# One core, layer norm + linear attention + MLP: the written order of all engines laid out anew from the third K product on

## The chip, the cores and the metric

One core of one Trainium2 chip. The metric is the device time of one execution in microseconds (us), the median over runs. Profiles show one profiled execution, with times from its first instruction.

## The reference

2048 rows of 512 features in bf16, 32 heads of 16, a hidden layer of 1792:

```python
def _A_ref(x, wqkv, wo):
    qkv = (x @ wqkv).reshape(B, S, 3, H, Dh).transpose(2, 0, 3, 1, 4)
    q, k, v = qkv[0], qkv[1], qkv[2]
    phi = lambda t: jnp.where(t > 0, t + 1, jnp.exp(t)) + 1e-6
    pq, pk = phi(q), phi(k)
    kv = jnp.einsum("bhsd,bhse->bhde", pk, v)
    z = jnp.einsum("bhsd->bhd", pk)
    num = jnp.einsum("bhqd,bhde->bhqe", pq, kv)
    den = jnp.einsum("bhqd,bhd->bhq", pq, z)[..., None] + 1e-6
    return (num / den).transpose(0, 2, 1, 3).reshape(B, S, D) @ wo
...
h = x + _A_ref(_layernorm(x), A_wqkv, A_wo)
h2 = h + relu(_layernorm(h) @ B_w1) @ B_w2
```

## The kernel before

The rows are cut into 16 tiles t of 128 rows, and four tiles make a chunk c of 512 columns for the transposed side. Nothing is planned at run time: the whole program is one list of words, ORDER, and a loop at the end calls for each word the function op_name with its numbers. A word stands for the work of one engine, and each engine runs its own words in the order of the list. Semaphores between engines are put in from the data that words share, also where a word writes a buffer that an earlier word has still to read. So moving a word changes what it stands behind on its own engine, and nothing else.

The words by stage (number after the name: tile, chunk and column block; the last number is often the PSUM bank or how many blocks the word covers):

- Loads on SyncE's queue: lx (x, L201), lk, lq, lv, lo, l1, l2 (weights, L204).
- First layer norm: S, A on VectorE (statistics, L222, L223), R on ScalarE (two instructions, L228), N on VectorE (L247). Its transpose into lnT is either T on TensorE with E on ScalarE (L266, L276), or X, a DMA transpose on SyncE (L287). One chunk's four tiles share one lnT.
- K products: K on TensorE, four matmuls (L295); phi in parts: F (exp) and U (relu) on ScalarE (L313, L316), M (min) and D (add) on VectorE (L320, L323). W (L328) does U and D in one VectorE instruction that reads PSUM. Then G on TensorE (L347) sums ln'phi(k) over the tiles into banks 4 to 7, and za, zf, z, zc, zh make the row sums z.
- Q products: Q (L303), with qF, qU, qM, qD, qW as for K, into pqT, one per chunk.
- gA (ScalarE, L380) or gD (VectorE, L383) copy G's banks, two at a time, into gT; kv (L388), kx (L396), m (L400) and mA (L403) make the matrix that stands for kv and wo together.
- Denominator of chunk c: dn on TensorE (16 small matmuls, L444), dnl (Ln, L450) and dnx (Exp spread over 16 columns, L457) on ScalarE, into rn, which is wk_sb used again. Per tile it is transposed into rd by dt, a DMA transpose on SyncE (L476), or by rt on TensorE (L266) with a copy by re on ScalarE (L468) or rv on VectorE (L472). dm on VectorE (L480) multiplies pqT with rd into pqs. rd exists once: dt of the next chunk writes what dm of this chunk reads. For chunk 0 the tiles 0, 1 and 2 go by dt, tile 3 by rt.
- h on TensorE (L490), hD on VectorE (L496, adds x); second layer norm s, a, r, n; x, a DMA transpose on SyncE (L288), back into lnT.
- MLP: p on TensorE (L506, first product), pA on ScalarE or pD on VectorE (relu, L512, L517), two banks each; f on TensorE (L526, second product, in two halves of seven), fo on VectorE (L534, adds h), fd the store (SyncE). There are two buffers for the hidden activations, for even and odd chunks.

All eight PSUM banks are one tile named bk, and a word's bank number says which bank it takes. The last tile's second product, f.15, is cut in three column pieces (15.3.1, 15.0.2, 15.2.1), each with its own fo and fd.

```python
    op_X = lambda t: nc.sync.dma_start_transpose(out=lnT_of(t), in_=ln_nat[:, t, :])
...
    def op_dt(t):
        j = t % CT
        nc.sync.dma_start_transpose(out=rd[:, :, j * P : (j + 1) * P], in_=rn[:, j, :])
...
    for word in ORDER.split():
        name, *idx = word.split(".")
        ops[name](*map(int, idx))
```

Of the kernel before, what the change touches and what calls it, by code (L numbers as in the profile page):

```python
# [16 lines left out]

ORDER = """
const table lx.0.1 lx.2.1 S.0 lx.1.1 S.2 A.0 S.1 A.2 R.0.1 N.0 R.2.1 lx.3.1 lk.0.2 lx.4.2 warm.1.7 warm.9.7
A.1 R.1.1 T.0.6 S.3 N.2 N.1 A.3 E.0 lk.2.2 warm.1.7 R.3.1 S.4 T.2.7 lx.6.2 E.2 N.3 S.5 T.1.4 A.4 K.0.1 E.1 A.5  # L20
F.0.1 R.4.2 S.6 T.3.2 K.1.0 M.0.1 E.3 U.0.1 lx.8.4 K.2.3 F.1.1 N.5 masks U.1.1 N.4 S.7 D.0.1 M.1.1 A.7 A.6
R.6.2 D.1.1 K.3.2 F.2.1 F.3.1 U.2.1 U.3.1 S.9 N.6 lx.12.4 X.5 G.0 X.4 G.1 M.2.1 A.9 S.8 N.7 A.8 M.3.1 D.2.1
R.8.2 K.5.1 lq.0.2 D.3.1 N.9 K.4.0 F.4.2 X.6 S.13 N.8 X.7 G.2 A.13 S.12 M.4.2 X.9 A.12 G.3 U.4.2 R.12.2 K.6.2
X.8 D.4.2 K.7.3 N.12 S.10 S.11 N.13 G.4 K.9.1 K.8.0 F.6.2 U.6.2 A.11 M.6.2 A.10 X.12 R.10.2 D.6.2 X.13 N.11
S.15 N.10 A.15 za.2 U.8.2 F.8.2 S.14 M.8.2 A.14 G.5 G.6 G.7 X.11 K.12.0 X.10 K.13.1 K.11.3 R.14.2 lq.2.2 za.4
N.14 D.8.2 K.10.2 N.15 za.6 X.14 F.12.2 U.12.2 X.15 F.10.2 G.8 Q.0.0.0 Q.0.1.1 M.12.2 lv.2.2 l1.0.2 l1.2.2
lo.0.4 lv.0.2 U.10.2 K.14.2 G.9 K.15.3 D.12.2 M.10.2 za.8 D.10.2 qU.0.0.2 G.10 za.10 qF.0.0.2 F.14.2 qM.0.0.2
za.12 Q.0.2.0 Q.0.3.1 G.11 M.14.2 zf.12 qF.0.2.2 G.12 W.14.2 qM.0.2.2 l2.7.7 qD.0.0.2 G.13 z.1.2.14 z.3.2.14
z.2.2.14 z.0.2.14 zc qW.0.2.2 G.14 G.15 zh dn.0.0 dnl.0 dnx.0.0.2 gD.2.2 gD.0.2 Q.1.0.2 Q.1.1.3 Q.1.3.1 kv.2.4
kv.3.4 dnx.0.3.1 dnx.0.2.1 kv.1.4 kv.0.4 Q.1.2.0 kx qF.1.0.2 qU.1.0.2 m.0.4 rt.3.3 m.2.6 m.1.5 Q.2.0.2 m.3.7  # L30
dt.1 qM.1.0.2 qF.1.2.2 dt.0 dt.2 re.3 qD.1.0.2 Q.2.1.3 mA.0.2 qM.1.2.2 l2.0.7 mA.2.2 qW.1.2.2 dn.1.5 dm.0.0.2
Q.2.3.1 dnl.1 dnx.1.0.2 dm.0.2.2 h.3.5 hD.3 dnx.1.2.2 qF.2.0.2 qU.2.0.2 s.3 h.1.4 hD.1 a.3 s.1 h.0.5 Q.2.2.0
n.3 hD.0 dt.5 dt.6 h.2.4 qU.2.2.2 qF.2.2.2 a.1 s.0 dt.7 hD.2 n.1 s.2 a.0 n.0 dt.4 dm.1.0.2 Q.3.0.2 Q.3.1.3
Q.3.3.1 Q.3.2.0 dm.1.2.2 a.2 x.3 h.4.6 h.7.4 qU.3.0.2 qF.3.0.2 x.1 h.6.5 h.5.7 qF.3.2.2 n.2 qM.2.2.2 qM.2.0.2
qD.2.0.2 qM.3.0.2 qD.2.2.2 x.0 dn.2.3 x.2 dnl.2 dnx.2.2.2 p.0.0.2 p.0.1.3 hD.4 qM.3.2.2 qW.3.2.2 qD.3.0.2
pD.0.0.2 hD.7 hD.5 dnx.2.0.2 p.0.3.1 dn.3.6 p.0.2.0 dt.10 dt.11 hD.6 s.5 s.4 dt.8 dt.9 p.0.5.3 p.0.4.2
dm.2.2.2 s.7 a.7 dm.2.0.2 r.0.4 pA.0.2.2 dnl.3 pA.0.4.2 p.0.7.1 p.0.6.0 dnx.3.2.2 pA.0.6.2 p.0.13.3 f.0.4.0.7
p.0.12.2 pA.0.12.2 f.1.5.0.7 h.9.3 h.10.1 h.11.0 h.8.6 dnx.3.0.2 a.4 s.6 hD.9 a.5 a.6 hD.10 hD.11 p.0.9.3
p.0.11.1 p.0.8.2 p.0.10.0 dt.14 dt.13 dt.15 f.3.7.0.7 pA.0.10.2 pA.0.8.2 n.5 dt.12 n.6 dm.3.0.2 dm.3.2.2 n.4
s.11 n.7 hD.8 h.14.1 h.13.3 f.0.4.7.7 h.12.0 h.15.6 hD.14 s.10 s.8 s.14 hD.12 s.9 x.5 x.7 x.6 x.4 f.1.5.7.7  # L40
f.3.7.7.7 fo.0 hD.15 p.1.9.1 p.1.8.0 f.2.6.0.7 pA.1.8.2 f.2.6.7.7 p.1.0.0 p.1.1.1 fo.1 a.14 a.10 a.8 fo.3 s.12
a.11 a.12 s.15 a.15 n.11 hD.13 s.13 a.13 a.9 n.8 n.10 p.1.3.3 n.9 n.12 pA.1.0.2 fo.2 x.10 fd.3 x.9 x.8 x.11
p.1.10.6 p.1.4.0 p.1.7.5 fd.0 p.1.5.1 p.1.2.2 p.1.11.7 p.1.6.4 n.14 pD.1.6.2 r.12.4 pA.1.4.2 n.15 n.13
pD.1.10.2 pA.1.2.2 p.2.4.0 p.2.5.1 pA.2.4.2 x.15 f.5.5.0.7 p.2.0.0 p.2.1.1 p.2.2.2 p.2.3.3 pA.2.0.2 p.1.13.1
f.7.7.0.7 p.1.12.0 f.4.4.0.7 pD.2.2.2 pD.1.12.2 p.2.7.3 p.2.6.2 p.2.13.1 f.6.6.0.7 f.7.7.7.7 f.5.5.7.7
p.2.12.0 r.4.4 pD.2.6.2 p.2.10.2 f.6.6.7.7 pA.2.12.2 x.12 x.14 x.13 fd.1 fd.2 p.2.9.1 p.2.11.3 p.2.8.0 fo.7
pA.2.10.2 pD.2.8.2 f.4.4.7.7 p.3.3.3 p.3.9.1 p.3.8.0 fo.4 pA.3.8.2 fo.5 fo.6 f.8.4.0.7 p.3.5.1 p.3.4.0 p.3.2.2
f.9.5.0.7 pD.3.4.2 pD.3.2.2 fd.5 fd.4 p.3.0.0 f.10.6.0.7 f.9.5.7.7 f.10.6.7.7 p.3.6.2 p.3.7.3 p.3.1.1 fd.6
f.8.4.7.7 pD.3.6.2 pA.3.0.2 r.8.4 fo.9 fo.10 p.3.13.1 f.11.7.0.7 p.3.11.3 p.3.12.0 pA.3.12.2 fo.8 f.11.7.7.7
fd.7 fd.9 p.3.10.2 f.12.4.0.7 f.14.6.0.7 fo.11 pD.3.10.2 f.15.5.0.14.3.1 f.12.4.7.7 f.14.6.7.7 fd.8 fd.10  # L50
fd.11 fo.15.3.1 fo.12 fo.14 f.13.5.0.7 f.13.5.7.7 fo.13 f.15.7.0.14.0.2 fd.12 fd.14 fd.13 fd.15.3.1
f.15.4.0.14.2.1 fo.15.0.2 fd.15.0.2 fo.15.2.1 fd.15.2.1
"""


# [521 lines left out]
```

## Time and profile before

| | |
|---|---|
| median of 3 runs | 170.41 us (170.32 to 170.6) |
| the profiled execution | 171.34 us, of which the span is 169.6 |
| TensorE (PE), matmuls | 162.6 us busy, 96% of the span |
| VectorE (DVE) | 102.6 us, 61% |
| ScalarE (ACT) | 65.2 us, 38% |
| GpSimd (POOL) | 4.9 us, 3% |
| DMA engines | 15.75 MB, mean 93 GB/s |
| mean granted TensorE clock | 1.000 |

The page gives busy time, the chain that ended last, and groups of instructions by line. In the chain and the timeline a row is: start, duration, what. PEld is the loading of weights, which goes beside the matmuls; SPq is SyncE's queue, where DMAs are issued one after the other. Of the DMA queues, q1 carries the kernel's transfers, and q8 and q14 carry packets of instructions for the engines' own fetching: seven of 16 KB on q8, 19 to 28 us apart in this trace, and four smaller ones on q14. A DMA's row on SPq is its issue alone; its landing is told in the DMA view as time from issue to landing.

### The profile page before, as it was taken

What the parts mean: (1) busy time and instruction counts of PE and PEld (TensorE: products, weight loads), DVE (VectorE), ACT (ScalarE), POOL (GpSimd) and SP (SyncE); (2) the same over time, 40 slices, a digit from 0 to 9 for tenths busy, and PEclk for the clock granted to TensorE, in tenths of its full rate; (3) what the DMA queues carried; (4) which work ended last, traced back from release to release, by engine and by line L of the source; (5) the groups of instructions that cost most, each with busy time, mean ns of one, the idle gap of its engine ahead of it and who ended that gap; (6) DMA issues with size and microseconds to landing.
All of it is one profiled execution on the core that took longest, in us unless ns stands there. A gap on an engine that the chain in (4) does not pass through costs nothing.

```text
span 169.6 us, 2272 instructions
## 1 busy us (share of the span) xinstructions
PE 162.6 (96%) x847; PEld 75.6 (45%) x863; DVE 102.6 (61%) x203; ACT 65.2 (38%) x98; POOL 4.9 (3%) x21
## 2 busy tenths in 40 slices
PE   7879989999999999999999999999999999999993
PEld 2334434445544354444444444444444444444553
DVE  3979999998678999545888903324204250344232
ACT  3868767741998827740400134320022200301000
POOL 7400000000000000000000000000000000000000
PEclk9999999999999999999999999999999999999999
DMA  4955545898357533314370052340000300020012
GB/s 128 312 192 142 110 81 125 270 395 261 65 122 203 108 64 66 62 31 95 60 69 0 9 115 62 69 120 1 0 0 0 124 0 4 0 93 31 0 66 62
DMA packets 31675, 15.75 MB, mean 93 GB/s; under 512 B 24240, under 2 KB 30640, under 8 KB 31664
## 3 DMA queue, kind: packets, MB, share of 16 engines
q1 hardware_dynamic: 31664, 15.61, 36.1%
q8 instruction: 7, 0.11, 0.3%
q14 instruction: 4, 0.03, 0.1%
HBM read 7.86 MB, written 2.10 MB: 59 GB/s over the span
## 4 chain that ended last, share of the span: by engine, by line
PE 83%; DMA 7%; DVE 5%; SPq 2%; issue 2%; ACT 0%; DVEq 0%
PE bk L526 28%; PE bk L506 28%; PE bk L490 9%; PE bk L303 6%; PE bk L347 6%; PE bk L295 4%; DMA x_nat<-in_A_x_dram 3%; DMA lnT<-h_nat 2%; DVE st L222 2%; DMA rd<-wk_sb 2%; SPq L201 1%; DVE h_nat L247 1%; DVE eb L320 1%; PE bk L444 1%; PE bk L388 1%
## 5 line engine op out<-in xcount | busy, mean ns | idle before, releaser
L526 PE MATMUL bk<-w_sb,at 128*128 128x512 bf16 (+2 forms) x248 | 51.2, 355 | 0.2
L506 PE MATMUL bk<-lnT,w_sb 128*128 128x512 bf16 x220 | 50.9, 380 | 0.2
L512 ACT ACTIVATE at<-bk 128x1024 bf16<-128x1024 f32 x17 | 17.2, 1022 | 67.3 <-PE bk L506 60.9
L526 PEld LDWEIGHTS <-at 128*128 128x128 bf16 x252 | 23.5, 98 | 25.2
L506 PEld LDWEIGHTS <-w_sb 128*128 128x128 bf16 x224 | 21.7, 98 | 26.0
L517 DVE TENSOR_SCALAR at<-bk 128x1024 bf16<-128x1024 f32 x11 | 13.4, 1223 | 32.7 <-PE bk L506 32.6
L534 DVE SCALAR_TENSOR_TENSOR gT<-bk,rstd,h_nat 128x512 bf16<-128x512 f32 (+2 forms) x18 | 12.0, 688 | 15.9 <-PE bk L526 14.8
L313 ACT ACTIVATE eb<-bk 128x1024 bf16<-128x1024 f32 (+1 forms) x18 | 16.4, 924 | 4.0 <-PE bk L295 2.4
L295 PE MATMUL bk<-wk_sb,lnT 128*128 128x512 bf16 x63 | 15.3, 380 | 0.7 <-DMA lnT<-h_nat 0.5
L490 PE MATMUL bk<-m_sb,pqs 128*128 128x512 bf16 x61 | 15.1, 380 | 0.2
L303 PE MATMUL bk<-lnT,wq_sb 128*128 128x512 bf16 x61 | 14.6, 379 | 0.1
L496 DVE TENSOR_TENSOR h_nat<-bk,x_nat 128x512 bf16<-128x512 f32 x16 | 10.8, 684 | 4.7 <-PE bk L490 4.7
L316 ACT ACTIVATE rb<-bk 128x1024 bf16<-128x1024 f32 (+1 forms) x14 | 12.5, 901 | 2.6 <-PE bk L303 1.9
L347 PE MATMUL bk<-at,h_nat 128*128 128x512 bf16 x56 | 13.4, 379 | 0.1
L222 DVE BATCH_NORM_STATS2 st<-x_nat 128x6 f32<-128x512 bf16 x16 | 10.7, 677 | 3.1 <-DMA x_nat<-in_A_x_dram 3.1
L224 DVE BATCH_NORM_STATS2 st<-h_nat 128x6 f32<-128x512 bf16 x16 | 10.7, 682 | 0.1
L347 PEld LDWEIGHTS <-h_nat 128*128 128x128 bf16 x64 | 6.2, 98 | 8.7 <-issue 1.5
L490 PEld LDWEIGHTS <-pqs 128*128 128x128 bf16 x64 | 5.9, 98 | 8.7 <-DVE pqs L480 2.0
L295 PEld LDWEIGHTS <-lnT 128*128 128x128 bf16 x64 | 6.0, 98 | 8.3 <-DMA lnT<-h_nat 1.4
L303 PEld LDWEIGHTS <-wq_sb 128*128 128x128 bf16 x64 | 6.1, 97 | 6.9
L457 ACT ACTIVATE wk_sb<-ld 128x1024 bf16<-128x1024 f32 (+1 forms) x9 | 8.2, 951 | 0.1
L480 DVE TENSOR_TENSOR pqs<-pqT,rd 128x1024 bf16<-128x1024 bf16 x8 | 5.2, 685 | 4.4 <-DMA rd<-wk_sb 2.6
(57 smaller groups left out, 89.9 us busy)
## 6 DMA issues: line engine op xcount, KB each, us to landing
w_sb<-in_B_w_dram SPq DMA_DIRECT2D x4, 896.0 KB, 5.8
out_dram<-gT SPq DMA_DIRECT2D x15, 128.0 KB, 1.9
x_nat<-in_A_x_dram SPq DMA_DIRECT2D x2, 512.0 KB, 7.5
x_nat<-in_A_x_dram SPq DMA_DIRECT2D x4, 128.0 KB, 2.3
wk_sb<-in_A_wqkv_dram SPq DMA_DIRECT2D x2, 256.0 KB, 3.3
...
```

The lines of the kernel that those rows point to most:

```text
L222: op_S = lambda t: nc.vector.bn_stats(out=st[:, t, :], in_=x_nat[:, t, :])
L295: nc.tensor.matmul(bk[:, b, :], lhsT=lnT[c][:, kd, j * P : (j + 1) * P], rhs=wk_sb[:, kd, :], start=(kd == 0), stop=(kd == KD - 1),)
L303: nc.tensor.matmul(bk[:, b, :], lhsT=wq_sb[:, kd, j * P : (j + 1) * P], rhs=lnT[c][:, kd, :], start=(kd == 0), stop=(kd == KD - 1),)
L313: nc.scalar.activation(out=buf(eb, kind, i, n), in_=bank(at_bank[kind, i], n), func=ACT.Exp)
L316: nc.scalar.activation(out=buf(rb, kind, i, n), in_=bank(at_bank[kind, i], n), func=ACT.Relu)
L347: nc.tensor.matmul(bk[:, KD + kd, :], lhsT=ln_nat[:, t, kd * P : (kd + 1) * P], rhs=pk(t)[:, 0, :], start=(t == 0), stop=(t == NT - 1),)
L490: nc.tensor.matmul(bk[:, b, :], lhsT=pqs[:, (c * KD + jb) % NQ, j * P : (j + 1) * P], rhs=m_sb[:, jb, :], start=(jb == 0), stop=(jb == KD ...
L506: nc.tensor.matmul(bk[:, b, cols], lhsT=w1_sb[:, kd, f * P : (f + 1) * P], rhs=lnT[c][:, kd, cols], start=(kd == 0), stop=(kd == KD - 1),)
L512: nc.scalar.activation(out=acts[c % 2][:, f : f + n, :], in_=bank(at_bank["p", c, f], n), func=ACT.Relu)
L517: nc.vector.tensor_scalar(out=acts[c % 2][:, f : f + n, :], in0=bank(at_bank["p", c, f], n), scalar1=0.0, scalar2=None, op0=ALU.max,)
L526: nc.tensor.matmul(bk[:, b, 0 : w * P], lhsT=acts[c % 2][:, f, j * P : (j + 1) * P], rhs=w2_sb[:, f, k * P : (k + w) * P], start=(f == 0), ...
L534: nc.vector.scalar_tensor_tensor(out=o_t[:, t % NO, cols], in0=bk[:, at_bank["f", t, k], 0 : w * P], scalar=rstd2[:, t : t + 1], in1=h_nat ...
```

## The change

ORDER is replaced from the word after K.0.1 on (the warm-up, the first transposes and K.0 stay; masks, which is GpSimd's own, is called earlier). A function op_warmq is added that no word calls. The matmuls are the same ones in another order, some in other banks. Twenty pieces of elementwise work change engine or form: W.6.2 for U.6.2 and D.6.2; U.14.2 and D.14.2 for W.14.2; qU.0.2.2 and qD.0.2.2 for qW.0.2.2; gA.0.2 for gD.0.2; rv.3 for re.3; and fifteen of the relu words of the MLP go from pA to pD or back. On SyncE, lx.12.4 goes before lx.8.4, lq.2.2, lq.0.2 and lv.2.2 go among other transposes, and both l2 loads before l1. The diff, the old lines up to the second chunk's denominators and the new ones up to the MLP's first product; of the rest, four new lines:

```diff
-A.1 R.1.1 T.0.6 S.3 N.2 N.1 A.3 E.0 lk.2.2 warm.1.7 R.3.1 S.4 T.2.7 lx.6.2 E.2 N.3 S.5 T.1.4 A.4 K.0.1 E.1 A.5
-F.0.1 R.4.2 S.6 T.3.2 K.1.0 M.0.1 E.3 U.0.1 lx.8.4 K.2.3 F.1.1 N.5 masks U.1.1 N.4 S.7 D.0.1 M.1.1 A.7 A.6
-R.6.2 D.1.1 K.3.2 F.2.1 F.3.1 U.2.1 U.3.1 S.9 N.6 lx.12.4 X.5 G.0 X.4 G.1 M.2.1 A.9 S.8 N.7 A.8 M.3.1 D.2.1
-R.8.2 K.5.1 lq.0.2 D.3.1 N.9 K.4.0 F.4.2 X.6 S.13 N.8 X.7 G.2 A.13 S.12 M.4.2 X.9 A.12 G.3 U.4.2 R.12.2 K.6.2
-X.8 D.4.2 K.7.3 N.12 S.10 S.11 N.13 G.4 K.9.1 K.8.0 F.6.2 U.6.2 A.11 M.6.2 A.10 X.12 R.10.2 D.6.2 X.13 N.11
-S.15 N.10 A.15 za.2 U.8.2 F.8.2 S.14 M.8.2 A.14 G.5 G.6 G.7 X.11 K.12.0 X.10 K.13.1 K.11.3 R.14.2 lq.2.2 za.4
-N.14 D.8.2 K.10.2 N.15 za.6 X.14 F.12.2 U.12.2 X.15 F.10.2 G.8 Q.0.0.0 Q.0.1.1 M.12.2 lv.2.2 l1.0.2 l1.2.2
-lo.0.4 lv.0.2 U.10.2 K.14.2 G.9 K.15.3 D.12.2 M.10.2 za.8 D.10.2 qU.0.0.2 G.10 za.10 qF.0.0.2 F.14.2 qM.0.0.2
-za.12 Q.0.2.0 Q.0.3.1 G.11 M.14.2 zf.12 qF.0.2.2 G.12 W.14.2 qM.0.2.2 l2.7.7 qD.0.0.2 G.13 z.1.2.14 z.3.2.14
-z.2.2.14 z.0.2.14 zc qW.0.2.2 G.14 G.15 zh dn.0.0 dnl.0 dnx.0.0.2 gD.2.2 gD.0.2 Q.1.0.2 Q.1.1.3 Q.1.3.1 kv.2.4
-kv.3.4 dnx.0.3.1 dnx.0.2.1 kv.1.4 kv.0.4 Q.1.2.0 kx qF.1.0.2 qU.1.0.2 m.0.4 rt.3.3 m.2.6 m.1.5 Q.2.0.2 m.3.7
-dt.1 qM.1.0.2 qF.1.2.2 dt.0 dt.2 re.3 qD.1.0.2 Q.2.1.3 mA.0.2 qM.1.2.2 l2.0.7 mA.2.2 qW.1.2.2 dn.1.5 dm.0.0.2
-Q.2.3.1 dnl.1 dnx.1.0.2 dm.0.2.2 h.3.5 hD.3 dnx.1.2.2 qF.2.0.2 qU.2.0.2 s.3 h.1.4 hD.1 a.3 s.1 h.0.5 Q.2.2.0
...
+A.1 R.1.1 T.0.6 S.3 N.2 N.1 masks A.3 E.0 lk.2.2 warm.1.7 R.3.1 S.4 T.2.7 lx.6.2 E.2 N.3 S.5 T.1.4 A.4 K.0.1
+E.1 lx.12.4 lx.8.4 K.2.3 T.3.0 A.5 F.0.1 R.4.2 S.6 E.3 M.0.1 N.5 U.0.1 X.5 K.1.2 S.7 D.0.1 F.1.1 K.3.0 A.7 A.6
+N.4 G.0 M.1.1 U.1.1 D.1.1 R.6.2 U.3.1 U.2.1 N.7 S.9 F.3.1 F.2.1 S.8 N.6 A.9 A.8 M.3.1 G.1 X.4 M.2.1 X.7 D.3.1
+X.6 R.8.2 D.2.1 N.9 N.8 S.12 S.13 K.5.1 S.10 A.13 A.12 K.4.0 G.2 X.9 X.8 F.4.2 U.4.2 R.12.2 K.7.3 K.6.2 G.3
+M.4.2 S.11 N.12 D.4.2 K.9.1 F.6.2 G.4 K.8.0 A.11 A.10 M.6.2 S.15 N.13 R.10.2 F.8.2 U.8.2 W.6.2 X.12 N.10 S.14
+N.11 A.14 M.8.2 A.15 D.8.2 lv.2.2 lq.2.2 X.13 G.5 X.10 X.11 lq.0.2 R.14.2 N.15 N.14 za.2 G.6 G.7 K.12.0 G.8
+za.4 K.13.1 K.10.2 K.11.3 F.12.2 U.12.2 G.9 F.10.2 X.15 X.14 U.10.2 Q.0.0.0 Q.0.1.1 qF.0.0.2 M.12.2 za.6 za.8
+qU.0.0.2 M.10.2 D.12.2 D.10.2 K.15.3 K.14.2 G.10 Q.0.3.1 Q.0.2.0 qM.0.0.2 G.11 lo.0.4 l2.7.7 lv.0.2 l2.0.7
+U.14.2 F.14.2 G.12 za.10 za.12 qF.0.2.2 qU.0.2.2 G.13 M.14.2 zf.12 D.14.2 qM.0.2.2 G.14 z.1.2.14 z.3.2.14
+z.0.2.14 z.2.2.14 l1.0.2 qD.0.2.2 qD.0.0.2 zc zh G.15 gA.0.2 dn.0.0 dnl.0 dnx.0.0.2 dnx.0.2.1 gD.2.2 Q.1.1.3
+Q.1.0.2 qU.1.0.2 kv.3.4 kv.2.4 kv.0.4 kv.1.4 qF.1.0.2 kx Q.1.3.1 Q.1.2.0 qM.1.0.2 qD.1.0.2 dnx.0.3.1 m.3.7
+rt.3.3 qF.1.2.2 dt.1 dt.0 dt.2 rv.3 m.0.4 m.1.5 m.2.6 l1.2.2 qM.1.2.2 Q.2.1.3 mA.0.2 qW.1.2.2 mA.2.2 Q.2.0.2
+dn.1.5 dnl.1 Q.2.3.1 dm.0.0.2 dm.0.2.2 h.3.6 hD.3 h.1.7 s.3 hD.1 dnx.1.0.2 Q.2.2.0 h.0.4 dnx.1.2.2 qF.2.0.2
+qU.2.0.2 a.3 s.1 hD.0 a.1 n.3 Q.3.0.2 h.2.5 s.0 hD.2 n.1 a.0 s.2 n.0 dt.5 dt.7 dt.6 dt.4 dm.1.0.2 dm.1.2.2 a.2
+qU.2.2.2 qF.2.2.2 Q.3.2.0 Q.3.3.1 Q.3.1.3 n.2 qF.3.2.2 r.0.4 qF.3.0.2 qU.3.0.2 h.5.6 h.4.4 x.3 x.1 qM.2.0.2
+qM.2.2.2 x.0 qD.2.0.2 qM.3.2.2 qM.3.0.2 qD.2.2.2 qW.3.2.2 qD.3.0.2 h.6.5 h.7.7 x.2 dn.2.3 dnl.2 p.0.0.2
...
+p.2.12.0 p.2.13.1 f.7.7.0.7 pA.2.6.2 r.4.4 fo.4 pD.2.12.2 fo.5 p.2.9.1 f.7.7.7.7 p.2.10.2 f.6.6.7.7 p.2.8.0
+p.2.11.3 fd.4 x.13 fd.5 fd.3 x.15 fo.7 fo.6 pA.2.8.2 pA.2.10.2 fd.7 fd.6 r.12.4 x.14 f.11.7.0.7 f.8.4.0.7
...
```

More of the change, by code (lines that the diff above doesn't have):

```diff
@@ L29 @@
-z.2.2.14 z.0.2.14 zc qW.0.2.2 G.14 G.15 zh dn.0.0 dnl.0 dnx.0.0.2 gD.2.2 gD.0.2 Q.1.0.2 Q.1.1.3 Q.1.3.1 kv.2.4
-kv.3.4 dnx.0.3.1 dnx.0.2.1 kv.1.4 kv.0.4 Q.1.2.0 kx qF.1.0.2 qU.1.0.2 m.0.4 rt.3.3 m.2.6 m.1.5 Q.2.0.2 m.3.7
-dt.1 qM.1.0.2 qF.1.2.2 dt.0 dt.2 re.3 qD.1.0.2 Q.2.1.3 mA.0.2 qM.1.2.2 l2.0.7 mA.2.2 qW.1.2.2 dn.1.5 dm.0.0.2
-Q.2.3.1 dnl.1 dnx.1.0.2 dm.0.2.2 h.3.5 hD.3 dnx.1.2.2 qF.2.0.2 qU.2.0.2 s.3 h.1.4 hD.1 a.3 s.1 h.0.5 Q.2.2.0
-n.3 hD.0 dt.5 dt.6 h.2.4 qU.2.2.2 qF.2.2.2 a.1 s.0 dt.7 hD.2 n.1 s.2 a.0 n.0 dt.4 dm.1.0.2 Q.3.0.2 Q.3.1.3
@@ L34 @@
[L34 to L52, printed above, removed]
+A.1 R.1.1 T.0.6 S.3 N.2 N.1 masks A.3 E.0 lk.2.2 warm.1.7 R.3.1 S.4 T.2.7 lx.6.2 E.2 N.3 S.5 T.1.4 A.4 K.0.1
+E.1 lx.12.4 lx.8.4 K.2.3 T.3.0 A.5 F.0.1 R.4.2 S.6 E.3 M.0.1 N.5 U.0.1 X.5 K.1.2 S.7 D.0.1 F.1.1 K.3.0 A.7 A.6
@@ new lines @@
+dn.1.5 dnl.1 Q.2.3.1 dm.0.0.2 dm.0.2.2 h.3.6 hD.3 h.1.7 s.3 hD.1 dnx.1.0.2 Q.2.2.0 h.0.4 dnx.1.2.2 qF.2.0.2
+qU.2.0.2 a.3 s.1 hD.0 a.1 n.3 Q.3.0.2 h.2.5 s.0 hD.2 n.1 a.0 s.2 n.0 dt.5 dt.7 dt.6 dt.4 dm.1.0.2 dm.1.2.2 a.2
+qU.2.2.2 qF.2.2.2 Q.3.2.0 Q.3.3.1 Q.3.1.3 n.2 qF.3.2.2 r.0.4 qF.3.0.2 qU.3.0.2 h.5.6 h.4.4 x.3 x.1 qM.2.0.2
+qM.2.2.2 x.0 qD.2.0.2 qM.3.2.2 qM.3.0.2 qD.2.2.2 qW.3.2.2 qD.3.0.2 h.6.5 h.7.7 x.2 dn.2.3 dnl.2 p.0.0.2
+p.0.3.1 p.0.1.3 hD.7 hD.5 s.5 dn.3.6 p.0.2.0 dnx.2.0.2 dnx.2.2.2 pA.0.0.2 dnl.3 pA.0.2.2 hD.6 s.6 p.0.5.3
@@ new lines @@
+p.0.4.2 dt.9 dt.10 dt.11 dt.8 s.7 a.6 pD.0.4.2 hD.4 p.0.6.0 p.0.7.1 pA.0.6.2 p.0.12.2 dm.2.2.2 p.0.13.3
+dnx.3.2.2 dnx.3.0.2 dm.2.0.2 a.7 p.0.11.1 p.0.10.0 s.4 a.4 a.5 h.8.6 h.10.4 h.11.7 dt.14 dt.13 n.7 hD.8 n.6
+dt.12 n.4 n.5 pA.0.10.2 pA.0.12.2 s.8 dt.15 f.2.6.0.7 p.0.9.3 x.5 x.7 x.4 h.9.0 p.0.8.2 hD.10 s.10 a.8 n.8
+hD.11 a.10 s.11 pD.0.8.2 f.1.5.0.7 dm.3.2.2 dm.3.0.2 f.2.6.7.7 f.1.5.7.7 h.12.4 fo.2 a.11 fo.1 h.14.2 hD.12
+s.12 hD.9 x.6 h.15.6 h.13.3 f.3.7.0.7 p.1.8.0 p.1.9.1 n.11 pA.1.8.2 hD.15 s.9 a.12 hD.14 a.9 s.14 n.9 s.15
@@ new lines @@
+n.10 hD.13 n.12 x.9 fd.2 x.12 fd.1 x.11 x.10 f.3.7.7.7 p.1.1.1 x.8 p.1.3.3 p.1.0.0 p.1.7.5 a.14 pD.1.0.2
+p.1.2.2 p.1.5.1 f.0.4.0.7 p.1.4.0 pA.1.4.2 s.13 f.0.4.7.7 pA.1.2.2 fo.0 a.13 a.15 fo.3 p.2.5.1 p.2.4.0 p.2.2.2
+p.1.6.4 p.1.11.7 pD.1.6.2 pD.2.4.2 p.2.3.3 p.1.10.6 p.2.0.0 p.2.1.1 f.4.4.0.7 fd.0 n.15 pD.2.0.2 n.13 n.14
+pA.1.10.2 pA.2.2.2 p.1.13.1 p.2.6.2 p.1.12.0 pD.1.12.2 f.6.6.0.7 p.2.7.3 f.5.5.0.7 f.5.5.7.7 f.4.4.7.7
+p.2.12.0 p.2.13.1 f.7.7.0.7 pA.2.6.2 r.4.4 fo.4 pD.2.12.2 fo.5 p.2.9.1 f.7.7.7.7 p.2.10.2 f.6.6.7.7 p.2.8.0
@@ new lines @@
+p.2.11.3 fd.4 x.13 fd.5 fd.3 x.15 fo.7 fo.6 pA.2.8.2 pA.2.10.2 fd.7 fd.6 r.12.4 x.14 f.11.7.0.7 f.8.4.0.7
+f.10.6.0.7 p.3.9.1 p.3.3.3 p.3.8.0 p.3.2.2 f.9.5.0.7 pA.3.2.2 r.8.4 pA.3.8.2 f.9.5.7.7 p.3.4.0 p.3.5.1 p.3.6.2
+pD.3.4.2 p.3.7.3 f.10.6.7.7 p.3.1.1 p.3.0.0 f.8.4.7.7 fo.9 fo.10 fo.8 pA.3.0.2 pA.3.6.2 p.3.12.0 f.11.7.7.7
+p.3.13.1 p.3.11.3 p.3.10.2 pA.3.10.2 f.14.6.0.7 pD.3.12.2 fo.11 f.15.5.0.14.3.1 f.12.4.0.7 f.14.6.7.7 fd.8
+f.12.4.7.7 fd.9 fd.11 fd.10 fo.15.3.1 fo.12 fo.14 f.13.5.0.7 f.13.5.7.7 f.15.7.0.14.0.2 fo.13 fo.15.0.2
@@ L53 @@
+fd.15.3.1 fd.14 fd.12 fd.13 f.15.4.0.14.2.1 fd.15.0.2 fo.15.2.1 fd.15.2.1
 """
@@ L215, in op_warm, with op_warmq @@
             nc.tensor.matmul(bk[:, b, :], lhsT=zeros[:, 0:P], rhs=zeros, start=True, stop=True)
+    def op_warmq(n, b):
+        for _ in range(n):
+            nc.tensor.matmul(bk[:, b, 0:P], lhsT=zeros[:, 0:P], rhs=zeros[:, 0:P], start=True, stop=True)
     def op_warms(n, b):
```

## The prediction, made before the changed kernel was run

> **What bounds the kernel now.** I read the page's busy times first, then TensorE's waits, the chain that ended last, then SyncE's transposes.
>
> ```profile
> PE 162.6 (96%) x847; PEld 75.6 (45%) x863; DVE 102.6 (61%) x203; ACT 65.2 (38%) x98; POOL 4.9 (3%) x21
> q8 instruction: 7, 0.11, 0.3%
> q14 instruction: 4, 0.03, 0.1%
> ```
>
> TensorE is full, so only its idle time can be won. Its own waits after the warm-up are three:
>
> ```profile
> PE bk L347 <- DVE pk_lo L323: 1.2, 1, 1.2
> PE bk L295 <- DMA lnT<-h_nat: 0.5, 1, 0.5
> PE bk L266 <- DVE h_nat L247: 0.3, 1, 0.3
> ```
>
> The chain of waits shows where else time is set:
>
> ```profile
> 18.02 0.31 DVE eb L320
> 18.33 3.38 DMA lnT<-h_nat
> 21.71 0.05 issue
> 21.75 1.04 PE bk L295 x4
> ...
> 46.53 3.04 DMA rd<-wk_sb
> 49.58 0.04 DVEq L480
> 49.62 0.04 issue
> 49.66 0.70 DVE pqs L480
> 50.36 0.05 issue
> 50.41 3.08 PE bk L490 x12
> ```
>
> K.8.0 (21.75) waits for transpose X.8; h.3 (50.41) for dt.2. In the timeline eight transposes follow on SyncE, back to back:
>
> ```profile
> 51.03 5.13 SPq L476 DMA_TRANSPOSE rd<-wk_sb  x4
> 56.26 5.16 SPq L288 DMA_TRANSPOSE lnT<-hn  x4
> ```
>
> The last, x.2, is issued at 60.19 and lands 2.4 us later at 62.63; p.0.0, which reads all of lnT0, starts at 62.68. From there TensorE has no gap over 0.1 us until its last matmul, at 166.7: 104.0 us of matmuls that are the same set before and after. Words of f.15 at the end, their stores and the 2.9 us of tail are the same too. So the change in time is the shift of p.0.0 plus any new gap behind it.
>
> **The change part by part.** The matmul set is unchanged; 0.216 us is the step between two 512-column matmuls, 0.86 us one word of four. Other rules read off the trace: a result of TensorE is taken 0.2 us after its end, a result of VectorE or ScalarE 0.05 us after, and instructions queued on VectorE overlap by 0.08 us, on ScalarE by 0.1 us.
>
> *Front, to K.8.0.* S.6 starts at 9.88 in both (its load lands at 9.85). The new VectorE order puts S.7 and D.0.1 ahead of N.4: S.6 0.69, M.0.1 0.28, N.5 0.41, S.7 0.69, D.0.1 0.41, less four overlaps, end at 12.02 instead of 12.34, so G.0 starts 0.32 earlier. But D.2.1 now follows D.3.1 (16.11 for 15.77) and G.2 waits for it until 16.16 (before: 15.89). D.4.2 has S.10, S.11 and N.12 ahead of it, 0.69 + 0.68 + 0.41 less three overlaps and the 0.1 gap that stood before D.4.2 until now, and ends at 20.58 instead of 19.14: G.4 moves from 19.35 to 20.63. N.8 sits before S.12 and S.13, and no load of wq before it on SyncE, so X.8 goes out at 17.77 for 18.33. It lands by 21.2 even with the 3.4 us of before, under G.4, which ends at 21.50. K.8.0 starts there: 0.25 earlier. W.6.2 in place of U.6.2 and D.6.2 ends at 23.13, just before G.6 (23.23). The 19.4 us of matmuls from K.8.0 to the end of G.15 (21.75 to 41.16) then end at 40.90. U.14.2/D.14.2 and qU.0.2.2/qD.0.2.2 for W.14.2 and qW.0.2.2 take ScalarE time that was idle (1.6 us before qF.0.2.2, 4.1 before dnl.0); D.14.2 ends at 38.66, G.14 is due at 38.77.
>
> *gA.0.2 for gD.0.2.* It frees 1.2 us of VectorE, where kx no longer is late, but on ScalarE it stands ahead of dnl.0: 1.03 us by mA (1038 ns). ScalarE runs gA 41.10, dnl.0 (0.37), dnx.0.0.2 (1.06), dnx.0.2.1 (0.61), qU.1.0.2 (1.01), qF.1.0.2 (1.00), dnx.0.3.1 (0.61), and ends at 46.34; before, dnx.0.3.1 was done at 43.71. TensorE comes to rt.3.3 at 46.08 (from 40.90: dn 0.62, four Q words 3.45, kv 0.89, m.3.7 0.22) and waits 0.31.
>
> *rv.3 for re.3.* The copy of 512 bf16 columns out of PSUM moves to VectorE, which the trace doesn't show. Bounds: 0.40 (L247, one bf16 source in SBUF) and 0.69 (L396, 512 columns from PSUM). Nearest is the PSUM copy L383: 1.22 for 1024 columns, so 0.6. rt.3.3 ends at 46.61, the three m words at 47.26, rv.3 at 47.45; Q.2.1.3 needs its bank and starts at 47.50. Q.2.1 and Q.2.0 take 1.73, so dn.1.5 starts at 49.23 for 48.81. dnl.1 follows its start by 0.71 as before (49.94) and dnx.1.0.2 ends 1.45 later, at 51.39. dt.5 goes out at 51.42 instead of 51.03: **0.39 later**. The eight transposes behind it keep their 1.3 us spacing (n.3, n.1, n.0 and n.2 are done before their slots), so x.2 and p.0.0 move by 0.39, to 63.07. TensorE is there at 62.9, so the rest is idle. [...]
>
> *dt.1, dt.0, dt.2.* dt.1 goes out at 43.51 for 43.22 (dnx.0.0.2 ends later). The packets of instructions matter here: dt.1 took 4.0 us and dt.0 and dt.2 over 3, where 2.4 is the median.
>
> ```profile
> q8 instruction: 1, 0.02, 3.6%
> rd<-wk_sb SPq DMA_TRANSPOSE x2, 3.5
> ```
>
> These lines of the DMA view for 44.4 to 46 show the packet, at 45.07. [...] dt.2, without l2.0.7 behind it, lands at 49.6 at the latest; qW.1.2.2 ends at 49.1, dm.0.2.2 by 50.95. That is earlier than dnx.1.0.2 at 51.39, so it no longer sets dt.5. A wait is removed and another takes its place.
>
> *Behind p.0.0.* I followed each bank and buffer. The closest: p.0.5.3 waits for pA.0.0.2 with 0.2 us to spare, p.2.9.1 for pD.2.12.2 with 0.05, f.2.6.7.7 for pD.0.8.2 with its second matmul. x.14 stands behind fd.4, fd.5, fd.7 and fd.6 on SyncE, so behind fo.6 (130.1); it lands at 133.3 and p.3.9.1 is due at 135.7. All that costs nothing. fd.15.3.1 ahead of fd.14, fd.12 and fd.13 leaves the last two stores in place.
>
> *Sum.* The last matmul ends 0.39 later. The profiled execution took 171.34 (span 169.6 and 1.74 around it), so 171.7 profiled; against the median of the runs, 170.41, that is **170.8**.
>
> **Rivals.**
>
> *A short rv.3.* At 0.40 to 0.45 and with no gap between the queued VectorE steps, the shift is 0.1 to 0.3: 170.5 to 170.7, no change. For it: L247. Against it: the source is PSUM.
>
> *A packet in the loads.* lv.2.2 and lq.2.2 now go out just before X.13, at 21.3 and 21.9, and a packet comes at about 22.6 (22.9 before). Before, X.13 alone with the packet took 4.1 us for 2.4, and X.11's issue 1.75 for 1.2. With 0.5 to 1 us of loads ahead, X.13 lands at 26.2 to 26.9 (due 26.7), X.11 at 27.5 to 28.6 (due 28.4), lq.0.2 at 29.3 to 30.4 (due 30.1). It decides once SyncE is held over 0.5 us; price 0.2 to 0.7 on top of 0.4: 171.0 to 171.5. [...]
>
> *An earlier front (faster).* VectorE stood idle 1.19 us before S.6, for the load lx.6.2, whose last part landed 2.4 us after its first. The loads behind it change places (lx.12.4 before lx.8.4). If the straggler comes 0.7 us earlier, all of the front, up to dt.5, moves with it, less 0.1 for X.8: 170.8 - 0.6 = 170.2, and with the full 1.19, 169.7. It decides from 0.75 to 0.85 on: the 0.39 has to be paid back, and 0.34 more to be told from no change. Against it: lx.6.2 is issued before the two that are exchanged.
>
> *A wait behind p.0.0* (x.14 over 2.4 us late, or pD.2.12.2): 0.3 to 1.0 on top, 171.1 to 171.8.
>
> **How the numbers follow.** This kernel's runs spread by 0.16%, so 0.2% (0.34 us) is about what can be told from no change: 170.07 and 170.75 are the bounds. Chances: the forecast 0.40 (170.65 to 171.0, of which 0.29 above 170.75), short rv.3 0.17 (same), packet 0.17 (slower), earlier front 0.18 (0.15 of it faster, the rest same), wait behind p.0.0 0.08 (slower). Sum: faster 0.15, same 0.31, slower 0.54. The range reaches from the earlier front's middle, 169.9, to the upper ends of the two slower rivals, 171.6.
>
> **What would show it.** Right: G.0 at 12.1, K.8.0 at 21.5, dnx.0.3.1 ending at 46.3 with a wait of rt.3.3 on it, dt.5 at 51.4 released by ScalarE rather than by dm.0.2.2, p.0.0 at 63.1, and no TensorE gap from there on. Wrong: dt.5 before 51.0; K.13.1, K.11.3 or Q.0.0.0 waiting for a DMA; a gap over 0.2 us after p.0.0; S.6 before 9.5.

## The result, and the profile after

The changed kernel takes 173.4 us (median of 6 runs, 172.03 to 173.62) against 170.45 for the kernel before (6 runs, 170.32 to 170.87): a ratio of 1.0149, 95% interval 1.0125 to 1.0173. That is slower, and by 2.95 us where 0.4 was forecast; it lies above the range. Where a ratio below rests on fewer executions than are named, one that lay over 1.5% above the fastest of its kernel is left out: 174.46 us in e5 and 174.62 in e6, two of the experiments below. The profiled execution took 173.52, with a span of 171.8.

Two lines of the page, busy time by engine and the clock that TensorE was granted in 40 slices of the span:

```profile
PE 164.2 (96%) x863; PEld 76.1 (44%) x863; DVE 100.6 (59%) x202; ACT 67.1 (39%) x100; POOL 4.8 (3%) x21
PEclk9996999999999999999999999999999999999999
```

VectorE lost 2.0 us and ScalarE gained 1.9, as the exchanged words would have it. TensorE is busy for 1.6 us more, with the same 863 matmuls. Most of that is missing records: the trace of before holds 847 of the 863, and a second one of the same kernel (e8, below) holds all of them and 163.9 us. What is more than that shows in the fourth slice: there the granted clock was below 0.7. The mean over the span is 0.989.

TensorE's waits (total, times, longest), beside which the three of before were 1.2, 0.5 and 0.3:

```profile
PE bk L351 <- DVE pk_lo L327: 2.5, 2, 2.3
PE bk L270 <- DVE h_nat L251: 0.8, 2, 0.5
PE bk L510 <- issue: 0.2, 1, 0.2
```

Line numbers after are four higher, since op_warmq stands above. L351 is G: G.0 now waits 2.3 us for D.0.1; the other wait in that row, 0.16 us, is G.1's. No wait for a DMA transpose is left on TensorE, and behind p.0.0 (L510) there is no gap over 0.2. So all of the loss lies ahead of p.0.0, and the chain of waits shows where it starts. First the chain of before, then that after, where each leaves the loads:

```profile
4.12 5.74 DMA x_nat<-in_A_x_dram
9.85 0.02 issue
9.88 0.04 DVE st L222
```

```profile
4.12 7.13 DMA x_nat<-in_A_x_dram
11.25 0.02 issue
11.28 0.04 DVE st L226
```

Further on, that chain runs through G.1. The rows of G.0 before, and of D.0.1 and G.0 after, from the timeline:

```profile
12.39 1.89 PE L347 MATMUL bk<-pk_lo,h_nat 128*128 128x512 bf16 x7 [1.17 <-DVE pk_lo L323]
```

```profile
13.00 0.41 DVE L327 TENSOR_TENSOR pk_lo<-rb,eb 128x512 bf16<-128x512 bf16 x1
13.46 1.02 PE L351 MATMUL bk<-pk_lo,h_nat 128*128 128x512 bf16 x4 [2.33 <-DVE pk_lo L327]
```

The load is lx.6.2, tiles 6 and 7 of x. It is issued at 4.12 in both, ahead of every DMA that the change moved, and lands 1.40 us later. S.6 (L226) waits for it with all of VectorE's queue behind it, D.0.1 among that queue, and G.0 waits for D.0.1.

The clock, in windows of 2 us of the kernel after (length; busy time and count of PE, PEld, DVE, ACT, POOL; granted clock; DMA share; GB/s):

```profile
11.00:13.00 2.00, 0.13 (x1) 0.00 (x0) 1.73 (x4) 0.51 (x2) 0.00 (x0) 1.00 0.27 109
13.00:15.00 2.00, 1.37 (x5) 0.49 (x5) 1.90 (x9) 1.36 (x5) 0.00 (x0) 0.84 0.35 72
15.00:17.00 2.00, 2.00 (x6) 0.73 (x5) 2.00 (x8) 1.43 (x5) 0.00 (x0) 0.50 0.64 126
17.00:19.00 2.00, 2.00 (x9) 0.80 (x8) 2.00 (x6) 0.18 (x2) 0.00 (x0) 0.80 0.37 71
```

TensorE stands still from 11.13 to 13.46. By the trace's records of the granted clock, the clock falls to half at 14.37 and is back at 17.79; in the window at half, 6 matmuls fit where 11 do at full clock.

The stations of the profiled executions, with those of three experiments told below (us; the last column is the start of the last matmul):

| kernel | lx.6.2 lands | S.6 | G.0 | K.8.0 | G.15 | dn.1.5 | p.0.0 | last matmul |
|---|---|---|---|---|---|---|---|---|
| before | 9.85 | 9.88 | 12.39 | 21.75 | 40.29 | 48.81 | 62.68 | 166.70 |
| after | 11.25 | 11.28 | 13.46 | 23.95 | 42.48 | 51.12 | 64.86 | 168.90 |
| after, loads back (e1) | 9.10 | 9.13 | 11.32 | 20.81 | 39.35 | 47.99 | 61.71 | 165.74 |
| before, loads exchanged (e2) | 11.45 | 11.47 | 13.99 | 24.11 | 42.73 | 51.44 | 65.23 | 169.26 |
| after, gap filled (e3) | 10.84 | 10.87 | 13.93 | 22.56 | 41.10 | 49.74 | 63.47 | 167.51 |

From S.6 to the last matmul it is 156.82 us before and 157.62 after, but 156.61 in e1 and 156.64 in e3, where the clock stays up. So the 2.20 us by which the last matmul moved are 1.40 of load, about 1.0 of clock (157.62 less 156.61 or 156.64) and about -0.2 of everything else that the order does. The two profiled executions differ by 2.18 us, the medians by 2.95: that of before, at 171.34, lies 0.9 above its median. An earlier landing of lx.6.2 in the other executions, such as e1's 9.10, would account for that; their traces do not exist, so it is only argued.

### The profile page after: what moved, and what is told of

It is laid out like the page before. It is cut to its first block, busy times and chain, and to the rows that moved or that the text cites. A ratio compares the mean times of both kernels' runs of the same rounds, so it can differ in the third digit from the quotient of the medians.

```text
span 171.8 us, 2286 instructions
## 1 busy us (share of the span) xinstructions
PE 164.2 (96%) x863; PEld 76.1 (44%) x863; DVE 100.6 (59%) x202; ACT 67.1 (39%) x100; POOL 4.8 (3%) x21
## 4 chain that ended last, share of the span: by engine, by line
PE 90%; DMA 4%; SPq 2%; DVE 1%; issue 1%; ACT 0%
PE bk L510 28%; PE bk L530 28%; PE bk L307 8%; PE bk L494 8%; PE bk L351 8%; PE bk L299 6%; DMA x_nat<-in_A_x_dram 4%; SPq L201 1%; PE bk L448 1%; PE bk L392 1%; SPq L204 1%; PE bk L404 1%; DVE pk_lo L327 0%; DVE st L226 0%; PE bk L370 0%
## 5 line engine op out<-in xcount | busy, mean ns | idle before, releaser
L510 PE MATMUL bk<-lnT,w_sb 128*128 128x512 bf16 x224 | 51.5, 379 | 0.2 <-issue 0.2
L516 ACT ACTIVATE at<-bk 128x1024 bf16<-128x1024 f32 x18 | 17.9, 1021 | 69.7 <-PE bk L510 69.7
L510 PEld LDWEIGHTS <-w_sb 128*128 128x128 bf16 x224 | 21.8, 98 | 26.2 <-issue 0.2
L521 DVE TENSOR_SCALAR at<-bk 128x1024 bf16<-128x1024 f32 x10 | 12.2, 1224 | 28.0 <-PE bk L510 28.0
L299 PE MATMUL bk<-wk_sb,lnT 128*128 128x512 bf16 x64 | 16.2, 392 | 0.1
L307 PE MATMUL bk<-lnT,wq_sb 128*128 128x512 bf16 x64 | 15.3, 378 | 0.0
L351 PE MATMUL bk<-at,h_nat 128*128 128x512 bf16 x56 | 13.5, 379 | 0.0
L320 ACT ACTIVATE rb<-bk 128x1024 bf16<-128x1024 f32 (+1 forms) x15 | 13.3, 906 | 0.0
L226 DVE BATCH_NORM_STATS2 st<-x_nat 128x6 f32<-128x512 bf16 x16 | 10.5, 679 | 4.4 <-DMA x_nat<-in_A_x_dram 4.4
L351 PEld LDWEIGHTS <-h_nat 128*128 128x128 bf16 x64 | 6.3, 99 | 10.4 <-issue 3.6
L324 DVE TENSOR_SCALAR eb<-eb 128x1024 bf16<-128x1024 bf16 (+1 forms) x18 | 6.7, 387 | 1.2 <-ACT eb L317 1.0
```

Of the source, the lines that this page charges most:

```text
L299: nc.tensor.matmul(bk[:, b, :], lhsT=lnT[c][:, kd, j * P : (j + 1) * P], rhs=wk_sb[:, kd, :], start=(kd == 0), stop=(kd == KD - 1),)
L307: nc.tensor.matmul(bk[:, b, :], lhsT=wq_sb[:, kd, j * P : (j + 1) * P], rhs=lnT[c][:, kd, :], start=(kd == 0), stop=(kd == KD - 1),)
L320: nc.scalar.activation(out=buf(rb, kind, i, n), in_=bank(at_bank[kind, i], n), func=ACT.Relu)
L351: nc.tensor.matmul(bk[:, KD + kd, :], lhsT=ln_nat[:, t, kd * P : (kd + 1) * P], rhs=pk(t)[:, 0, :], start=(t == 0), stop=(t == NT - 1),)
L510: nc.tensor.matmul(bk[:, b, cols], lhsT=w1_sb[:, kd, f * P : (f + 1) * P], rhs=lnT[c][:, kd, cols], start=(kd == 0), stop=(kd == KD - 1),)
L516: nc.scalar.activation(out=acts[c % 2][:, f : f + n, :], in_=bank(at_bank["p", c, f], n), func=ACT.Relu)
```

## The experiments

My theory after seeing the trace was: the exchange of lx.12.4 and lx.8.4 delays lx.6.2, and the gap that this opens costs the clock. The rival was that the exchange is innocent and that the order itself (D.0.1, gA, rv.3) costs.

**The loads put back (e1).** The kernel after, with one pair of words exchanged:

```diff
-E.1 lx.12.4 lx.8.4 K.2.3
+E.1 lx.8.4 lx.12.4 K.2.3
```

> The changed kernel with lx.8.4 issued before lx.12.4 again, nothing else. Theory 1 (the exchange of the two loads keeps the load lx.6.2 ahead of them from finishing): lx.6.2 lands at 9.7 to 10.2 as before, not at 11.25; S.6 starts by 10.2, G.0 by 12.5, the TensorE clock stays at 1.00 in the windows from 13 to 19 (0.84, 0.50, 0.80 in the changed kernel), and the time is 170.4 to 171.0 (the prediction's sum with rv.3 at the measured 0.42). Rival (the load's landing varies by itself from program to program, whatever stands behind it): S.6 still starts at 11 or later, and the time stays between 172 and 173.6.

Measured: 170.94 (12 runs) against 171.19 for the kernel before on the same chip (23 runs), ratio 0.9986, interval 0.9963 to 1.0008. All of the loss is gone with one pair of words. The load lands 0.6 us earlier than the earliest that was expected:

```profile
4.12 4.98 DMA x_nat<-in_A_x_dram
9.10 0.02 issue
9.13 0.12 DVE st L226
```

The same load is 2.15 us shorter than after. The 2.3 us wait of G.0 is gone: the two rows of L351 that TensorE's waits still have are G.2's (at) and G.1's (pk_lo), at 15.54 and 12.50:

```profile
PE bk L351 <- DVE at L327: 0.2, 1, 0.2
PE bk L351 <- DVE pk_lo L327: 0.2, 1, 0.2
```

**The loads exchanged in the kernel before (e2).** The converse, with nothing else of the change:

```diff
-U.0.1 lx.8.4 K.2.3
+U.0.1 lx.12.4 lx.8.4 K.2.3
...
-N.6 lx.12.4 X.5
+N.6 X.5
```

> The kernel before with lx.12.4 issued just before lx.8.4, nothing else. Theory 1: lx.6.2 lands at 10.8 or later for 9.85, G.0 moves from 12.39 to 13.4 or later, TensorE stands idle 2.3 us or more before it, its clock falls in some executions, and the time is 171.4 to 173. Rival (landing varies by itself): as before, 170.3 to 170.9.

Measured: 174.02 (6 runs) against 171.19, ratio 1.0153, interval 1.0113 to 1.0193: the whole loss, from this pair alone, and 1.0 us more than the 173 that was expected at most. Its chain (line numbers here are one lower than before), and its windows around the gap:

```profile
4.12 7.33 DMA x_nat<-in_A_x_dram
11.45 0.02 issue
11.47 0.04 DVE st L221
```

```profile
13.00:15.00 2.00, 1.01 (x3) 0.40 (x3) 2.00 (x8) 0.64 (x3) 0.00 (x0) 0.66 0.35 72
15.00:17.00 2.00, 2.00 (x6) 0.68 (x5) 2.00 (x9) 1.91 (x5) 0.00 (x0) 0.50 0.48 89
```

Late load and half clock are both there. From S.6 to the last matmul it takes 157.79, which is 0.97 more than before. So the loss goes when the pair is put back in the kernel after (e1), and comes when the pair alone is exchanged in the kernel before (e2).

**The gap filled (e3).** To part load and clock, the kernel after with six more matmuls, of zeros, into bank 7, which nobody holds then:

```diff
-K.3.0 A.7 A.6
+K.3.0 warm.6.7 A.7 A.6
```

> The changed kernel with six matmuls of zeros (1.3 us at full clock) between K.3.0 and G.0, where TensorE stood idle for 2.5 us. They add no work to the result. Theory 2 (the idle time makes the clock fall to 0.5 for 3.4 us, and that costs about 1 us of its own, since G.4 then starts 0.7 us after D.4.2 is done instead of with it): S.6 is as late as in the changed kernel, the clock stays at 1.00, K.5.1 and K.4.0 run at 0.216 us a matmul, and the time is 172.0 to 172.6 with less spread. Rival (the slow matmuls are hidden behind VectorE's chain to D.4.2): within 0.3 of the changed kernel's 173.4.

Measured: 172.75 (6 runs, 172.13 to 173.1) against 171.19, ratio 1.0086, interval 1.0058 to 1.0115. The load is late still (10.84), the clock is 1.000 in all six executions, and about two fifths of the loss are won back (a ratio of 1.0086 for 1.0149). The time is 0.15 us above the range that was expected. The windows:

```profile
13.00:15.00 2.00, 2.00 (x11) 0.88 (x9) 1.90 (x8) 1.94 (x6) 0.00 (x0) 1.00 0.49 94
15.00:17.00 2.00, 2.00 (x11) 0.93 (x10) 2.00 (x9) 1.17 (x4) 0.00 (x0) 1.00 0.53 103
```

Eleven matmuls now lie in the window that held six. In this profile TensorE also waits 1.4 us for wk in K.0.1, and with the six matmuls it comes to G.0 3.06 us behind S.6, where e1 has 2.19; at K.8.0 that is made up (11.69 for 11.68). The kernel after shows the price of the clock by itself, too: its four executions at 0.989 or 0.990 took 173.28 to 173.62, its two at 1.000 took 172.03 and 172.84.

**gD.0.2 back (e4).** Of the order's own costs the prediction's largest was gA.0.2 ahead of dnl.0. On top of e1:

```diff
-G.15 gA.0.2 dn.0.0
+G.15 dn.0.0
...
-gD.2.2 Q.1.1.3
+gD.2.2 gD.0.2 Q.1.1.3
```

> As e1_loads_back, with gD.0.2 on VectorE behind gD.2.2 in place of gA.0.2 on ScalarE. The prediction's step (gA.0.2 stands ahead of dnl.0 and makes rt.3.3 and dt.5 late): dnl.0 starts about 0.5 to 0.9 earlier relative to the end of G.15, rt.3.3 no longer waits for dnx.0.3.1, kx is 1.1 later, and p.0.0 and the time are 0.1 to 0.4 below e1_loads_back. Rival (the step costs nothing, since the Q words behind it hold the time): within 0.1 of e1_loads_back, or above it, since kx and with it m.3.7 come later.

Measured: 171.54 (12 runs) against 171.19, ratio 1.002, interval 0.999 to 1.0051; no gain. In the trace rt.3.3 starts 6.30 us behind G.15's start where it is 5.91 in e1, and dn.1.5 8.93 for 8.64; p.0.0 starts 53.16 us behind S.6 for 52.58. That gA costs time here has fallen: by these two traces, and by the medians (0.60 us apart), it is rather gD that does.

**What delays lx.6.2 (e5, e6, e7, e9).** These change only the order of issues on SyncE. First a load of wq between lx.6.2 and the two others, on top of e1 (its old place, behind X.11, left empty):

```diff
-E.1 lx.8.4 lx.12.4
+E.1 lq.0.2 lx.8.4 lx.12.4
...
-X.11 lq.0.2
+X.11
```

> As e1_loads_back, with the load lq.0.2 (256 KB of wq, from its place behind X.11) issued between lx.6.2 and lx.8.4. Theory A (which addresses stand behind lx.6.2 decides: lx.8.4 is the next 4 KB of the same rows, lx.12.4 lies 4 KB further): with rows of another tensor behind it lx.6.2 lands later than the 9.1 to 9.9 of the orders with lx.8.4, at 10.3 or more, and the time is over 171.5. Theory B (loads of x behind it hold it up, whichever they are, and lx.12.4 more): it lands earlier, at 8.2 to 9.0, S.6 starts by 9.0, and the time is 0.1 to 0.7 below e1_loads_back (170.9) unless S.9, which waits for lx.8.4 0.6 us longer, takes it back.

Measured: 170.83 (12 runs) against 170.87, ratio 0.9987, interval 0.9969 to 1.0004, and lx.6.2 lands at 9.21, in neither theory's window. So a load of another tensor directly behind it does not drag it, and does not speed it either: e1 has 9.10.

Then lx.6.2 ahead of the second load of wk, on top of e1:

```diff
-E.0 lk.2.2 warm.1.7 R.3.1 S.4 T.2.7 lx.6.2 E.2
+E.0 lx.6.2 lk.2.2 warm.1.7 R.3.1 S.4 T.2.7 E.2
```

> As e1_loads_back, with lx.6.2 issued ahead of lk.2.2 (the second half of wk). If S.6's wait for lx.6.2 sets the front, as theory 1 has it: lx.6.2 lands at 7.4 to 8.9, S.6 starts 0.5 to 1.0 earlier; lk.2.2 lands at 8.0 to 9.0, K.0.1 and with it F.0.1 come 0.5 to 1.0 later, and M.0.1 becomes the wait. Time 170.2 to 170.7 against 170.9. Rival (K.0.1 takes over the whole gain or more): D.0.1 ends no earlier, time 170.9 to 171.6.

Measured: 173.66 (6 runs) against 170.87, ratio 1.0134, interval 1.0093 to 1.0175. lx.6.2 lands earlier (8.77), but wk lands at 9.75, and TensorE waits for it:

```profile
PE bk L299 <- DMA wk_sb<-in_A_wqkv_dram: 2.0, 1, 2.0
```

The rival was right, and by more than its price: the gap in K.0.1 costs the clock as well, which is at half from 9.92 to 13.33.

Then lx.12.4 later, behind X.5, on top of e1:

```diff
-E.1 lx.8.4 lx.12.4 K.2.3
+E.1 lx.8.4 K.2.3
...
-X.5 K.1.2
+X.5 lx.12.4 K.1.2
```

> As e1_loads_back, with lx.12.4 issued behind X.5 (at about 11) and not at 5.1, so that lx.8.4 alone stands behind lx.6.2. Theory A (addresses): lx.6.2 lands as in e1_loads_back, 9.1 to 9.8, time within 0.3 of 170.9. Theory B (bytes of x behind it): it lands at 8.2 to 8.9, S.6 and all behind it start 0.3 to 0.9 earlier, time 170.1 to 170.6. lx.12.4 lands near 14 and S.12 is due at 16.

Measured: 172.61 (6 runs) against 170.87, ratio 1.0137, interval 1.0096 to 1.0178. lx.6.2 lands at 9.08, as in e1 (9.10): with lx.8.4 directly behind it, whether another 512 KB follow makes no difference. The loss is a new one. X.4 now stands behind lx.12.4 and lands at 16.90, where e1 has 14.22, and K.4.0 waits:

```profile
PE bk L299 <- DMA lnT<-h_nat: 2.1, 1, 2.1
```

Last, the two loads exchanged as in the kernel after, but with wq in between:

```diff
-E.1 lx.12.4 lx.8.4
+E.1 lq.0.2 lx.12.4 lx.8.4
...
-X.11 lq.0.2
+X.11
```

> The changed kernel, lx.12.4 still ahead of lx.8.4, with lq.0.2 issued between lx.6.2 and lx.12.4 (as e5_wq_between, but with the two loads of x exchanged). Theory C (lx.6.2 is held up only by a load of rows 12 to 15 issued directly behind it; with wq behind it, as with lx.8.4, it landed at 9.1 to 9.9): it lands at 9.0 to 10.0, the clock stays at 1.00, and the time is 170.5 to 171.3. Rival (lx.12.4 holds it up also from one place further back): lands at 10.5 or later, time 172 to 174.

Measured: 171.55 (12 runs) against 170.98, ratio 1.0028, interval 1.0005 to 1.005. lx.6.2 lands at 9.11, so tiles 12 to 15 do not delay it when another load goes between. The time is 0.25 us above the range that was expected. The chain shows a wait that e1 does not have: lx.8.4, now the last of the four, holds S.9 and S.8 until 13.36, where S.9 starts at 12.69 in e1:

```profile
5.62 7.71 DMA x_nat<-in_A_x_dram
13.36 1.29 DVE st L226 x2
```

**The kernel before once more (e8).**

> The kernel before, unchanged, for one more profile: where the landing of lx.6.2 stands from one execution to another. Theory 1: between 9.0 and 10.2, apart from the 10.8 to 11.5 of the three profiles with the exchanged loads. Rival (the landing varies as widely in one kernel): 10.5 or later.

Measured: 171.19, one execution, with lx.6.2 landing at 9.71 for 9.85 and 156.82 us from S.6 to the last matmul, the same to 0.01. So the way from S.6 on can be compared across executions, while the landing moved by 0.14 with the same code. Over all profiles, lx.6.2 lands at 11.25, 11.45 and 10.84 with lx.12.4 directly behind it, at 8.96 to 9.85 (six profiles) with lx.8.4, at 9.11 and 9.21 with wq. The line of the DMA view for 4.1 to 4.4 holds this one issue (KB, us from issue to landing), in e8 and after:

```profile
x_nat<-in_A_x_dram SPq DMA_DIRECT2D x1, 256.0 KB, 5.6
```

```profile
x_nat<-in_A_x_dram SPq DMA_DIRECT2D x1, 256.0 KB, 7.1
```

**rt.3.3 earlier (e10).** Does dnx.0.3.1, then rt.3.3 and rv.3, set dn.1.5, as the prediction has it? On top of e1, dnx.0.3.1 goes directly behind dnx.0.2.1, and rv.3 ahead of qM.1.0.2:

```diff
-dnx.0.2.1 gD.2.2
+dnx.0.2.1 dnx.0.3.1 gD.2.2
...
-Q.1.2.0 qM.1.0.2 qD.1.0.2 dnx.0.3.1 m.3.7 rt.3.3 qF.1.2.2
+Q.1.2.0 m.3.7 rt.3.3 rv.3 qM.1.0.2 qD.1.0.2 qF.1.2.2
...
-dt.2 rv.3 m.0.4
+dt.2 m.0.4
```

> As e1_loads_back, with dnx.0.3.1 right behind dnx.0.2.1 on ScalarE and rv.3 ahead of qM.1.0.2 and qD.1.0.2 on VectorE, so that rt.3.3 waits for nothing and Q.2.1.3 finds its bank free. The prediction's step (rt.3.3 waits for dnx.0.3.1, Q.2.1.3 for rv.3, and by them dn.1.5, dt.5 and p.0.0 are late): dn.1.5 starts 0.2 to 0.4 earlier after G.15 than the 8.64 of e1_loads_back, and the time is 0.2 to 0.4 lower. Rival (dn.1.5 waits for qW.1.2.2, which ends at 47.95 for a start at 47.99 and hangs on ScalarE's row of seven instructions from gA.0.2 to qF.1.2.2, whatever their order): dn.1.5 within 0.1 of 8.64 behind G.15, time within 0.2 of e1_loads_back.

Measured: 171.46 (12 runs) against 170.98, ratio 1.0028, interval 1.0004 to 1.0052: no gain, and by its interval a small loss. dn.1.5 starts 8.60 behind G.15, 8.64 in e1, and after two of its sixteen matmuls stands still, by the waits and the timeline:

```profile
DVE rd L476 <- PE bk L270: 1.5, 1, 1.5
PE bk L448 <- DVE pqT L332: 0.7, 1, 0.7
```

```profile
47.46 1.23 DVE L332 SCALAR_TENSOR_TENSOR pqT<-bk,eb 128x1024 bf16<-128x1024 f32 x1
48.74 0.50 PE L448 MATMUL bk<-zhd,pqT 128*128 128x8 bf16 x14 [0.74 <-DVE pqT L332]
```

dn.1.5 now waits for qW.1.2.2. But the edit itself made qW.1.2.2 late: rv.3, moved ahead of qM.1.0.2, keeps VectorE idle for 1.5 us until rt.3.3 is done, so that qM.1.0.2 starts 6.75 us behind G.15 (5.37 in e1) and qW.1.2.2 ends 9.49 behind it (8.60 in e1). So e10 does not part the two. What the trace of e1 shows is a tie: qW.1.2.2 ends at 47.95, with qM.1.2.2 started as soon as ScalarE's qF.1.2.2 was done, and dn.1.5 starts at 47.99, right behind TensorE's own row. An earlier rt.3.3 alone had nothing to win there, which bears the rival out at this point; its time, within 0.2 of e1, did not come.

No version beats the kernel before for certain: e1 and e5 have the lowest ratios, and the intervals of both hold 1.

## Why the prediction was wrong

**The step that failed** is the first of the front: "S.6 starts at 9.88 in both (its load lands at 9.85)". It starts at 11.28, and e1 and e2 show that the exchange of the two loads behind it does that. The rival *An earlier front* had named this very exchange as able to move lx.6.2, but gave it one sign, an earlier landing. The argument put against it, that lx.6.2 is issued first, was taken as a reason for no effect; issued first, it still landed at 11.25 for 9.85, by what was issued behind it. It should have had a price on both sides of nothing: the same straggler that could come 0.7 us sooner could come 1.4 us later.

**A term that was missing** is the clock. With S.6 late, TensorE's stop ahead of G.0 grows from 1.17 to 2.33 us, and four of six executions then have a granted clock of 0.989 or 0.990; in the profiled one it is at half for 3.41 us. In the profiles it costs 0.97 (e2 against before) to 1.01 us (after against e1). With the load back it did not come up: e1 ran at 0.998 or more in all twelve.

**The front's other steps** held, counted from S.6. Forecast were D.0.1's end 2.14 behind S.6, G.0 2.19, G.4 10.75 and K.8.0 11.62; e1 has 2.13, 2.19, 10.82 and 11.68. Against the kernel before K.8.0 is 0.19 earlier by that count, for 0.25.

**gA.0.2** was mis-sized. The sum had it start 0.2 behind the end of G.15. It reads banks 4 and 5 alone, which the first two of G.15's four matmuls complete, and starts at 39.98 in e1, ahead of that end (40.21); in the trace after, the second of the four ends at 43.08 and gA starts at 43.11. That makes 0.43 us, and with it the wait of rt.3.3 falls away; e4 shows the sign reversed.

**rv.3** was taken at 0.6, between 0.40 and 0.69. Measured, in the groups by form of the kernel after:

```profile
L476 DVE COPY rd<-bk 128x512 bf16<-128x512 bf16 x1 | 0.4, 417 | 0.0
```

That is the lower end. The choice of the nearest row, an f32 copy, was wrong: this copy of bf16 from PSUM took about as long as L247 with its bf16 source in SBUF (0.40), and not as long as L396 (0.69) or half of L383 (1.22 for 1024 columns), whose sources are f32 in PSUM.

**The sum of the order alone** was +0.39 at p.0.0; e1, counted from S.6, has -0.22, and dn.1.5 -0.07 for +0.42. From G.15's start to dn.1.5 the sum had 9.19 us, e1 has 8.64; the two mis-sized terms are 0.49 of that (the wait of rt.3.3, 0.31, and 0.18 of rv.3). The traces of e1 and e10 add a bar that the sum did not have on its path: qW.1.2.2, which ends 0.04 ahead of dn.1.5 in e1. That the forecast had the right sign, slower, is luck: its +0.39 did not come, and the loss came by a step that it had put at nothing.

**What held.** dt.5 no longer follows dm.0.2.2: after, it goes out at 53.19, just behind the end of dnx.1.0.2 at 53.16, and so ScalarE releases it. There is no new gap behind p.0.0. *A packet in the loads* did not come to pay: packets do fall among them after, at 21.56 and 23.73 (X.12 takes 4.0 us from issue to landing, lq.2.2 holds SyncE for 1.39 us), but K.13.1, K.11.3 and Q.0.0.0 wait for no DMA.

Of the signs that would show the prediction wrong, the list had "S.6 before 9.5" but no later S.6. The sign that came, S.6 at 11.28, was not on it.
